# softmax(q) of batches 2 to 7: block transposes on VectorE with exchanged half rows, in place of TensorE transposes

## The chip, the cores and the metric

One NeuronCore of a Trainium2 chip. The metric is the device time of one execution in microseconds; the kernel before has a median of 920.75 us over three runs (920.45 to 921.54). The profiled execution is another run of the same kernel.

## What is computed

Eight batches (B = 8) of eight heads (H = 8), 576 tokens (S) and 64 channels per head (D), followed by a feed-forward layer with squared relu. All inputs are drawn in float32, the two weights come as float64 words. Cut to what matters:

```python
q_s = softmax of q over the 64 channels of a head (max, exp, sum + 1e-9, divide)
k_s = softmax of k over the 576 tokens (max, exp, sum + 1e-9, divide)
kv  = einsum('bhsd,bhse->bhde', k_s, v)
att = einsum('bhsd,bhde->bhse', q_s, kv)
x   = att.transpose(0, 2, 1, 3).reshape(B * S, H * D)      # 4608 x 512
h   = maximum(x @ w_in, 0)                                  # w_in 512 x 2048
out = h * h @ w_out                                         # w_out 2048 x 512
```

## The kernel before

Every large product is done three times in 32-bit pieces: an operand is cut into a rounded high part (a ScalarE copy) and a low part (a subtraction on VectorE or GpSimd), and high x high, high x low and low x high are added in PSUM.

The outer loop (line 634) runs over t = 0 to 8. In round t the feed-forward layer works on 512 tokens of batch t (round 8 takes the last 64 tokens of all eight batches, kept in DRAM as x_tail), and the attention of batch b = t + 1 is done beside it. The feed-forward layer has NF = 16 steps f. A step issues `first(t, f)` (12 matmuls of 512 columns into a PSUM tile h, of which there are two), then ScalarE's relu r and VectorE's square in place (L478, L479), and later `second(f - 2)` (12 matmuls into the accumulators acc). `split_g(f)` makes the two parts gh (ScalarE, L487) and gl (VectorE, L488) that `second(f)` reads; it is issued in step f after `second(f - 2)` in the program, from step 2 on. The h tile of step f is free for `first(f + 2)` once gl of step f is done.

The heads are taken in four pairs p = 0 to 3. Pair p has the four steps f = 4p to 4p + 3, called quarters i = 0 to 3 here. `step` (line 590) is issued between first and second, `step_after` (line 601) after split_g:

- quarter 0: exp of q (ScalarE), then row sums, 1e-9, reciprocal and the scaling into qn (VectorE, `q_exp`, `q_norm`); for p = 0 the same for the 64 tail rows of all heads (`tail_norm`).
- quarter 1: exp of k; the loads of k and q of the next pair are issued on SP's queue.
- quarter 2: `tail_turn` (p = 0 only, two TensorE transposes of the tail), `kv_product` (10 matmul instructions, then VectorE and ScalarE make kv, kvh, kvl), and `q_turn` (four TensorE transposes of qn into PSUM, qh by ScalarE, ql by VectorE); then the loads of v.
- quarter 3: `x_product` (6 matmuls of 288 columns, copied to x), and `prepare(b, p + 1)`: the maxima of k over a partition's rows (VectorE), the maximum across partitions and the subtraction (GpSimd), the row maxima of q and their subtraction (VectorE, `q_max`). For the next batch's pair 0, `prepare` is issued after the 16 steps.

q is loaded with four consecutive tokens on each partition, both heads of the pair side by side (256 KB in pieces of 1 KB); the 64 tail tokens of all heads come in a load of their own. Token order in x is therefore (partition, c), and `store` writes the rows of out by "(p c) e -> p c e".

Round 0 and the start before it are ordered by a planner (a cost model of the engines decides the order of each engine's instructions). From round 1 on the order is that of the program text (`manual_schedule`, line 636), and every engine and SP's DMA queue run their instructions in that order: an instruction that waits holds up all behind it. In the start (lines 520 to 572), batch 0 is done pair by pair in stages; `k_max` writes the tile km, of which there are two, and a TensorE transpose (`k_turn_max`, L320) reads it.

Of the kernel before, what the change touches and what calls it, by code (L numbers as in the profile page):

```python
# [9 lines left out]
F32 = mybir.dt.float32  # L10
F32R = mybir.dt.float32r
# [3 lines left out]
AF = mybir.ActivationFunctionType  # L15
ALU = mybir.AluOpType
AX = mybir.AxisListType
# [5 lines left out]
def attention_ffn(  # L23
# [19 lines left out]

    nc = tc.nc
    B, H, S, D = q.shape
    DM = H * D
    DF = w_in.shape[1]
    P = 128  # L50
    C = 4
    M = C * P
# [6 lines left out]
    EPS = 1e-9  # L59
# [2 lines left out]
    LW = 2  # L62
    LD = 6
    SH = S // 2
    assert B * TL == M and DM == NP * P and C * P == M

    const = ctx.enter_context(tc.tile_pool(name="const", bufs=1))
# [105 lines left out]
    made = {}  # L173
# [15 lines left out]
    def load_kq(b, p, which, queue=nc.sync):  # L189
# [4 lines left out]
        )  # L194
        made[which, b, p] = t

    def load_v(b, p):
        t = pair_tile(b, p, [P, VW], "v")[:, 0:C * W].rearrange("p (c w) -> p c w", c=C)
        nc.gpsimd.memset(t[:, :, D:D + 1], 1.0)
        for j in range(2):  # L200
            nc.sync.dma_start(
                out=t[:, :, j * (D + 1):j * (D + 1) + D],
                in_=v[b, 2 * p + j, 0:M, :].rearrange("(p c) d -> p c d", c=C),
            )
        made["v", b, p] = t

    def load_tail_kq(b, which, queue=nc.sync):

        src = k if which == "k" else q
        t = (att if b else boot).tile(  # L210
            [P, G, D], F32, tag=f"{which}t", name=f"{which}t_{b}", bufs=1
        )
        for g in range(2):
            queue.dma_start(
                out=t[g * TL:(g + 1) * TL],
                in_=src[b, g * G:(g + 1) * G, M:S, :].rearrange("h p d -> p h d"),
            )
        made[f"{which}t", b] = t
# [10 lines left out]

    def load_tail(b):  # L230
        load_tail_kq(b, "k")
        load_tail_kq(b, "q")

    def small(shape, tag, name, bufs=2):
        pool = att if shape[-1] % 64 == 0 else tiny
        return pool.tile(shape, F32, tag=tag, name=name, bufs=bufs)
# [8 lines left out]
    def rows_norm(t, g, name, eng, out=None):  # L245
        sm = small([P, g], f"sm_{g}", f"sm_{name}")
        nc.vector.tensor_reduce(out=sm, in_=t, op=ALU.add, axis=AX.X)
        nc.vector.tensor_scalar_add(sm, sm, EPS)
        nc.vector.reciprocal(out=sm, in_=sm)
        by = sm.unsqueeze(2).broadcast_to([P, g, D])  # L250
        if out is not None:
            t, by = (a.rearrange("p (h c) d -> p h c d", h=2) for a in (t, by))
        eng.tensor_tensor(out=t if out is None else out, in0=t, in1=by, op=ALU.mult)

    def tail_exp(b):
        qt = made["qt", b]
# [26 lines left out]
    def k_max(b, p):  # L283
        kr = made["k", b, p]
        tl, th = tail_of(b, p)
        km = small([P, P], "km", f"km_{b}_{p}")
        nc.vector.tensor_reduce(  # L287
            out=km.rearrange("p (h d) -> p h d", h=2), in_=kr.rearrange("p h c d -> p h d c"),
            op=ALU.max, axis=AX.X,
        )  # L290
        nc.vector.tensor_tensor(  # L291
            out=km[tl], in0=km[tl], in1=made["kt", b][tl, th, :].rearrange("p h d -> p (h d)"),
            op=ALU.max,
        )
        made["km", b, p] = km
# [20 lines left out]
    def k_turn_max(b, p):  # L316

        km = made.pop(("km", b, p))
        ps = bank(f"kmT_{b}_{p}")
        nc.tensor.transpose(out=ps[:, 0:P], in_=km, identity=ident)  # L320
        kc = small([P, 1], "kc", f"kc_{b}_{p}")
        nc.vector.tensor_reduce(out=kc, in_=ps[:, 0:P], op=ALU.max, axis=AX.X)
        dg = small([P, P], "dg", f"dg_{b}_{p}")
        nc.vector.tensor_scalar(
            out=dg, in0=ident, scalar1=kc, scalar2=None, op0=ALU.mult
        )
        made["dg", b, p] = dg
# [20 lines left out]
    def q_max(b, p, eng):  # L348
        rows_max(made["q", b, p].rearrange("p h c d -> p (h c) d"), 2 * C, f"{b}_{p}", eng)
# [5 lines left out]
    def q_norm(b, p, eng):  # L355
        qr = made.pop(("q", b, p)).rearrange("p h c d -> p (h c) d")
        qn = pair_tile(b, p, [P, C, P], "qn")
        rows_norm(
            qr, 2 * C, f"{b}_{p}", eng, qn.rearrange("p c (h d) -> p h c d", h=2)
        )  # L360
        made["qn", b, p] = qn
# [138 lines left out]
    def store(t, acc, c):  # L500
        o = cvt.tile([P, DM], F32, tag="w", name=f"o_{t}_{c}")
        if t == B and c == C - 1:
            nc.vector.tensor_copy(out=o[:, 0:DM // 2], in_=acc[c][:, 0:DM // 2])
            nc.scalar.copy(out=o[:, DM // 2:DM], in_=acc[c][:, DM // 2:DM])
        elif c % 2:
            nc.scalar.copy(out=o, in_=acc[c])
        else:
            nc.vector.tensor_copy(out=o, in_=acc[c])
        if t < B:
            rows = out[t * S:t * S + M, :].rearrange("(p c) e -> p c e", c=C)  # L510
            nc.sync.dma_start(out=rows[:, c, :], in_=o)
        else:
            per = P // TL
            for j in range(per):
                r0 = (c * per + j) * S + M
                queue = nc.scalar if c == C - 1 and j % 2 else nc.sync
                queue.dma_start(out=out[r0:r0 + TL, :], in_=o[j * TL:(j + 1) * TL, :])
# [63 lines left out]
    def prepare(b, p):  # L581

        k_max(b, p)
        if b > 1:
            k_shift_pool(b, p)
        q_max(b, p, nc.vector if b > 1 else nc.gpsimd)
        if p == 0:
            tail_exp(b)

    def step(b, s):  # L590

        p, i = divmod(s, NP)
        if i == 0:
            if b == 1:
                k_turn_max(b, p)
            q_exp(b, p)
            q_norm(b, p, nc.vector if b > 1 else nc.gpsimd)
            if p == 0:
                tail_norm(b)

    def step_after(b, s, x):

        p, i = divmod(s, NP)
        if b == 1 and s in (1, 4, 8, 12):
            k_shift_pe(b, p)
            k_exp(b, p)
        elif b > 1 and i == 1:
            k_exp(b, p)
        if i == 1:
            if p + 1 < NP:  # L610
                load_kq(b, p + 1, "k")
                load_kq(b, p + 1, "q")
            elif b + 1 < B:
                load_kq(b + 1, 0, "k")
                load_kq(b + 1, 0, "q")
        elif i == 2:
            if p == 0:
                tail_turn(b)
            kv_product(b, p)
            q_turn(b, p)  # L620
            if p + 1 < NP:
                load_v(b, p + 1)
            elif b + 1 < B:
                load_v(b + 1, 0)
                load_tail(b + 1)
                load_tail_v(b + 1)
        elif i == 3:
            x_product(b, p, x)
            if p + 1 < NP:
                prepare(b, p + 1)  # L630
# [77 lines left out]
```

## Time and profile before

| | before |
|---|---|
| median of 3 runs | 920.75 us |
| profiled execution, its own time | 920.5 us |
| span from first to last instruction | 918.7 us |
| granted TensorE clock, mean | 0.992 of 2.4 GHz |
| TensorE (PE) busy | 880.0 us, 96% |
| weight loads (PEld) busy | 731.2 us, 80% |
| VectorE (DVE) busy | 502.4 us, 55% |
| ScalarE (ACT) busy | 348.9 us, 38% |
| GpSimd (POOL) busy | 154.7 us, 17% |
| time outside the span | 1.8 us |

Busy shares are means over the whole span. Matmuls are pipelined, so the duration of one matmul in a row (0.39 us for 512 columns) is longer than the distance from one start to the next (0.227 us); what a matmul costs is read from the distances. Rounds 1 to 6, in which the changed code runs, lie between about 156 and 742 us. In rows of the timeline, x2 or x8 counts merged instructions, and what stands in brackets is idle time of that engine just before and what ended it.

### The profile page before, as it was taken

What the parts mean: (1) busy time and instruction counts of PE and PEld (TensorE: products, weight loads), DVE (VectorE), ACT (ScalarE), POOL (GpSimd) and SP (SyncE); (2) the same over time, 40 slices, a digit from 0 to 9 for tenths busy, and PEclk for the clock granted to TensorE, in tenths of its full rate; (3) what the DMA queues carried; (4) which work ended last, traced back from release to release, by engine and by line L of the source; (5) the groups of instructions that cost most, each with busy time, mean ns of one, the idle gap of its engine ahead of it and who ended that gap; (6) DMA issues with size and microseconds to landing.
All of it is one profiled execution on the core that took longest, in us unless ns stands there. A gap on an engine that the chain in (4) does not pass through costs nothing.

```text
span 918.7 us, 11463 instructions
## 1 busy us (share of the span) xinstructions
PE 880.0 (96%) x4136; PEld 731.2 (80%) x4136; DVE 502.4 (55%) x982; ACT 348.9 (38%) x679; POOL 154.7 (17%) x238
## 2 busy tenths in 40 slices
PE   3598999999999999999999999999999999999997
PEld 2486778888888888888888888888888888888886
DVE  8978888654564447545745466454744442233222
ACT  3997445333343234333433343333423332232221
POOL 3366663101111111111111101111110100000000
PEclk9799999999999999999999999999999999999999
DMA  8990102111221122111311031112211020001001
GB/s 247 355 381 25 38 24 84 35 35 34 59 81 35 35 53 86 35 34 32 95 36 35 15 101 35 35 35 58 81 35 35 1 97 1 1 8 39 0 1 47
DMA packets 84937, 57.38 MB, mean 62 GB/s; under 512 B 53520, under 2 KB 78096, under 8 KB 84752
## 3 DMA queue, kind: packets, MB, share of 16 engines
q1 hardware_dynamic: 83168, 55.33, 19.6%
q10 hardware_dynamic: 1712, 1.31, 0.5%
q8 instruction: 33, 0.54, 0.2%
q14 instruction: 24, 0.20, 0.1%
HBM read 46.14 MB, written 10.49 MB: 62 GB/s over the span
## 4 chain that ended last, share of the span: by engine, by line
PE 81%; DVE 8%; ACT 7%; issue 2%; DMA 1%; POOL 1%; SPq 0%; DVEq 0%; ACTq 0%
PE h L473 38%; PE acc L495 37%; PE kv L391 2%; PE x L428 2%; PE qT L368 1%; DVE xl L464 1%; DVE gl L488 1%; ACT r L478 1%; DVE h L479 1%; ACT gh L487 1%; ACT raw_i L125 1%; ACT raw_i L126 1%; ACT raw_o L125 1%; DVE km L287 1%; ACT raw_o L126 1%
## 5 line engine op out<-in xcount | busy, mean ns | idle before, releaser
L473 PE MATMUL h<-xh,wi 128*128 128x512 f32 x1152 | 382.8, 395 | 5.3 <-ACT wi L152 5.0
L495 PE MATMUL acc<-wo,gh 128*128 128x512 f32 x1152 | 349.6, 390 | 3.5 <-ACT gh L487 3.4
L473 PEld LDWEIGHTS h<-xh,wi 128*128 128x128 f32 x1152 | 217.1, 189 | 53.1 <-ACT wi L152 5.9
L495 PEld LDWEIGHTS acc<-wo,gh 128*128 128x128 f32 x1152 | 215.1, 188 | 49.7 <-ACT gh L487 5.7
L473 PE MATMUL h<-xl,wi 128*128 128x512 f32 x576 | 225.7, 392 | 0.0
L495 PE MATMUL acc<-wo,gl 128*128 128x512 f32 x576 | 217.4, 389 | 0.0
L479 DVE SCALAR_TENSOR_TENSOR h<-h,r 128x512 f32<-128x512 f32 x144 | 100.6, 698 | 193.4 <-ACT r L478 192.7
L488 DVE TENSOR_TENSOR gl<-h,gh 128x512 fp32r<-128x512 f32 x144 | 99.5, 691 | 171.5 <-ACT gh L487 168.1
L478 ACT ACTIVATE r<-h 128x512 f32<-128x512 f32 x144 | 86.0, 597 | 219.2 <-PE h L473 219.1
L487 ACT ACTIVATE gh<-r 128x512 fp32r<-128x512 f32 x144 | 91.0, 632 | 196.8 <-PE acc L495 194.1
L495 PEld LDWEIGHTS acc<-wo,gl 128*128 128x128 f32 x576 | 108.0, 188 | 22.6
L473 PEld LDWEIGHTS h<-xl,wi 128*128 128x128 f32 x576 | 108.9, 189 | 20.8
L301 POOL TENSOR_TENSOR k<-k,kmx 128x512 f32<-128x512 f32 x24 | 31.0, 1291 | 172.6 <-issue 172.6
L313 POOL PARTITION_ALL_REDUCE kmx<-km x24 | 17.6, 734 | 226.8 <-DVE km L291 221.1
L391 PEld LDWEIGHTS kv<-v,ek 128*128 128x128 f32 x256 | 33.4, 195 | 4.5 <-ACT wi L152 2.4
L391 PE MATMUL kv<-v,ek 128*128 128x129 f32 x256 | 34.8, 279 | 2.2 <-ACT wi L152 2.0
L287 DVE TENSOR_REDUCE km<-k 128x128 f32<-128x512 f32 x32 | 33.9, 1059 | 2.7 <-DMA k<-in_k_dram 2.7
L342 ACT ACTIVATE ek<-k 128x512 f32<-128x512 f32 x32 | 20.1, 627 | 23.6 <-POOL k L301 16.7
L382 DVE TENSOR_TENSOR ql<-qT,qh 128x512 fp32r<-128x512 f32 x32 | 22.0, 688 | 6.8 <-ACT qh L381 6.8
L416 ACT CAST kvh<-kv 128x128 fp32r<-128x128 f32 x32 | 9.5, 298 | 39.3 <-DVE kv L406 39.1
L240 DVE TENSOR_REDUCE mx<-q 128x8 f32<-128x512 f32 x32 | 21.7, 679 | 2.7 <-DMA q<-in_q_dram 2.3
L464 DVE TENSOR_TENSOR xl<-x,xh 128x512 fp32r<-128x512 f32 x32 | 20.2, 687 | 5.4 <-ACT xh L463 5.3
(84 smaller groups left out, 675.2 us busy)
## 6 DMA issues: line engine op xcount, KB each, us to landing
k<-in_k_dram SPq DMA_DIRECT2D x32, 256.0 KB, 2.8
v<-in_v_dram SPq DMA_DIRECT2D x64, 128.0 KB, 3.1
raw_i<-in_moe_w_in_dram SPq DMA_DIRECT2D x16, 512.0 KB, 8.1
raw_o<-in_moe_w_out_dram SPq DMA_DIRECT2D x16, 512.0 KB, 7.9
out_dram<-o SPq DMA_DIRECT2D x32, 256.0 KB, 2.6
q<-in_q_dram SPq DMA_DIRECT2D x28, 256.0 KB, 2.9
q<-in_q_dram ACTq DMA_DIRECT2D x4, 256.0 KB, 4.7
kt<-in_k_dram SPq DMA_DIRECT2D x16, 64.0 KB, 2.7
```

The costliest lines, as they stand in the source:

```text
L240: nc.vector.tensor_reduce(out=mx, in_=t, op=ALU.max, axis=AX.X)
L287: nc.vector.tensor_reduce(out=km.rearrange("p (h d) -> p h d", h=2), in_=kr.rearrange("p h c d -> p h d c"), op=ALU.max, axis=AX.X,)
L301: eng.tensor_tensor(out=kr, in0=kr, in1=kmx.rearrange("p (h d) -> p h d", h=2).unsqueeze(2).broadcast_to([P, 2, C, D]), op=ALU.subtract,)
L382: nc.vector.tensor_tensor(out=ql[:, 0:M], in0=ps, in1=qh[:, 0:M], op=ALU.subtract)
L391: nc.tensor.matmul(out=ps[:, 0:W], lhsT=kr[:, c, :], rhs=vr[:, c, :], start=(c == 0), stop=False)
L464: nc.vector.tensor_tensor(out=lo, in0=src[:, p, :], in1=hi, op=ALU.subtract)
L473: nc.tensor.matmul(out=ps, lhsT=w[f][:, p * P:(p + 1) * P], rhs=m, start=(n == 0), stop=(n == 3 * NP - 1))
L478: nc.scalar.activation(out=r, in_=ps, func=AF.Relu)
L479: nc.vector.scalar_tensor_tensor(out=ps, in0=ps, scalar=0.0, in1=r, op0=ALU.max, op1=ALU.mult)
L487: nc.scalar.activation(out=gh, in_=r, func=AF.Square)
L488: nc.vector.tensor_tensor(out=gl, in0=ps, in1=gh, op=ALU.subtract)
L495: nc.tensor.matmul(out=acc[c], lhsT=a[:, cs], rhs=w[f], start=(f == 0 and n == 0), stop=(f == NF - 1 and n == 2),)
```

## The change

For batches b >= TB = 2 only. q of a pair is loaded by four DMAs into a tile of 128 partitions x 18 x 32: partition j*64 + a*32 + r holds, for head j and channel half a, the 32 channels of token 32 g + r, for g = 0 to 17, so that all 576 tokens are in it and the separate tail load of q is left out. A row of a head lies on two partitions, so row maxima and row sums of the halves are exchanged with four small SBUF-to-SBUF DMAs (`swap_halves`, 32 partitions x 72 bytes each) and joined. VectorE then transposes the tile in 32 x 32 blocks into 128 partitions (channels) x 576 tokens; ScalarE makes the high part, GpSimd the low part. Tail transposes, the copies of the tail and the TensorE transposes of q are not issued for these batches. Tokens of x are now in their natural order, so `store` writes "(c p) e -> p c e" for t >= 2. For all batches the tile km of `k_max` has one buffer in place of two.

By place: `blocks_max` stands in `prepare` (quarter 3 of the pair before), `blocks_exp` in quarter 0, `blocks_norm` in quarter 1 (both in `step`), `blocks_turn` in quarter 1 (in `step_after`, ahead of the loads of the next pair), `blocks_split` in quarter 2 (in `step`).

```diff
@@ -62,6 +64,9 @@
     LW = 2
     LD = 6
     SH = S // 2
+    TB = 2
+    Q = 32
+    NG = S // Q
     assert B * TL == M and DM == NP * P and C * P == M
 
     const = ctx.enter_context(tc.tile_pool(name="const", bufs=1))
@@ -194,6 +199,24 @@
         )
         made[which, b, p] = t
 
+    def load_q_blocks(b, p):
+
+        t = att.tile([P, NG, Q], F32, tag="q", name=f"q_{b}_{p}")
+        for j in range(2):
+            for a in range(2):
+                at = j * D + a * Q
+                nc.sync.dma_start(
+                    out=t[at:at + Q],
+                    in_=q[b, 2 * p + j, :, a * Q:(a + 1) * Q].rearrange("(g t) d -> t g d", t=Q),
+                )
+        made["q", b, p] = t
+
+    def load_q(b, p):
+        if b < TB:
+            load_kq(b, p, "q")
+        else:
+            load_q_blocks(b, p)
+
     def load_v(b, p):
         t = pair_tile(b, p, [P, VW], "v")[:, 0:C * W].rearrange("p (c w) -> p c w", c=C)
         nc.gpsimd.memset(t[:, :, D:D + 1], 1.0)
@@ -229,7 +252,8 @@
 
     def load_tail(b):
         load_tail_kq(b, "k")
-        load_tail_kq(b, "q")
+        if b < TB:
+            load_tail_kq(b, "q")
 
     def small(shape, tag, name, bufs=2):
         pool = att if shape[-1] % 64 == 0 else tiny
@@ -252,6 +276,58 @@
             t, by = (a.rearrange("p (h c) d -> p h c d", h=2) for a in (t, by))
         eng.tensor_tensor(out=t if out is None else out, in0=t, in1=by, op=ALU.mult)
 
+    def swap_halves(t, name):
+
+        o = small([P, NG], "sw", f"sw_{name}", 1)
+        for j in range(2):
+            for a in range(2):
+                at, of = j * D + a * Q, j * D + (1 - a) * Q
+                nc.sync.dma_start(out=o[at:at + Q], in_=t[of:of + Q])
+        return o
+
+    def blocks_max(b, p):
+        mx = small([P, NG], "bmx", f"bmx_{b}_{p}", 1)
+        nc.vector.tensor_reduce(out=mx, in_=made["q", b, p], op=ALU.max, axis=AX.X)
+        made["bmx", b, p] = mx, swap_halves(mx, f"m_{b}_{p}")
+
+    def blocks_exp(b, p):
+        t = made["q", b, p]
+        mx, sw = made.pop(("bmx", b, p))
+        nc.vector.tensor_tensor(out=mx, in0=mx, in1=sw, op=ALU.max)
+        nc.vector.tensor_tensor(
+            out=t, in0=t, in1=mx.unsqueeze(2).broadcast_to([P, NG, Q]), op=ALU.subtract
+        )
+        nc.scalar.activation(out=t, in_=t, func=AF.Exp)
+        sm = small([P, NG], "bsm", f"bsm_{b}_{p}", 1)
+        nc.vector.tensor_reduce(out=sm, in_=t, op=ALU.add, axis=AX.X)
+        made["bsm", b, p] = sm, swap_halves(sm, f"s_{b}_{p}")
+
+    def blocks_norm(b, p):
+        t = made["q", b, p]
+        sm, sw = made.pop(("bsm", b, p))
+        nc.vector.scalar_tensor_tensor(
+            out=sm, in0=sm, scalar=EPS, in1=sw, op0=ALU.add, op1=ALU.add
+        )
+        nc.vector.reciprocal(out=sm, in_=sm)
+        nc.vector.tensor_tensor(
+            out=t, in0=t, in1=sm.unsqueeze(2).broadcast_to([P, NG, Q]), op=ALU.mult
+        )
+
+    def blocks_turn(b, p):
+
+        t = made.pop(("q", b, p)).rearrange("p g d -> p (g d)")
+        qt = att.tile([P, S], F32, tag="qn", name=f"qT_{b}_{p}")
+        nc.vector.transpose(out=qt, in_=t)
+        made["qf", b, p] = qt
+
+    def blocks_split(b, p):
+        qt = made.pop(("qf", b, p))
+        qh = att.tile([P, S], F32R, tag="qh", name=f"qh_{b}_{p}", bufs=1)
+        ql = att.tile([P, S], F32R, tag="ql", name=f"ql_{b}_{p}", bufs=1)
+        nc.scalar.copy(out=qh, in_=qt)
+        nc.gpsimd.tensor_tensor(out=ql, in0=qt, in1=qh, op=ALU.subtract)
+        made["qT", b, p] = (qh, ql)
+
     def tail_exp(b):
         qt = made["qt", b]
         rows_max(qt, G, f"t{b}", nc.vector)
@@ -283,7 +359,7 @@
     def k_max(b, p):
         kr = made["k", b, p]
         tl, th = tail_of(b, p)
-        km = small([P, P], "km", f"km_{b}_{p}")
+        km = small([P, P], "km", f"km_{b}_{p}", 1)
         nc.vector.tensor_reduce(
             out=km.rearrange("p (h d) -> p h d", h=2), in_=kr.rearrange("p h c d -> p h d c"),
             op=ALU.max, axis=AX.X,
@@ -507,7 +583,9 @@
         else:
             nc.vector.tensor_copy(out=o, in_=acc[c])
         if t < B:
-            rows = out[t * S:t * S + M, :].rearrange("(p c) e -> p c e", c=C)
+            rows = out[t * S:t * S + M, :].rearrange(
+                "(p c) e -> p c e" if t < TB else "(c p) e -> p c e", c=C
+            )
             nc.sync.dma_start(out=rows[:, c, :], in_=o)
         else:
             per = P // TL
@@ -583,18 +661,27 @@
         k_max(b, p)
         if b > 1:
             k_shift_pool(b, p)
-        q_max(b, p, nc.vector if b > 1 else nc.gpsimd)
+        if b >= TB:
+            blocks_max(b, p)
+            return
+        q_max(b, p, nc.gpsimd)
         if p == 0:
             tail_exp(b)
 
     def step(b, s):
 
         p, i = divmod(s, NP)
-        if i == 0:
-            if b == 1:
-                k_turn_max(b, p)
+        if b >= TB:
+            if i == 0:
+                blocks_exp(b, p)
+            elif i == 1:
+                blocks_norm(b, p)
+            elif i == 2:
+                blocks_split(b, p)
+        elif i == 0:
+            k_turn_max(b, p)
             q_exp(b, p)
-            q_norm(b, p, nc.vector if b > 1 else nc.gpsimd)
+            q_norm(b, p, nc.gpsimd)
             if p == 0:
                 tail_norm(b)
 
@@ -607,17 +694,22 @@
         elif b > 1 and i == 1:
             k_exp(b, p)
         if i == 1:
+            if b >= TB:
+                blocks_turn(b, p)
             if p + 1 < NP:
                 load_kq(b, p + 1, "k")
-                load_kq(b, p + 1, "q")
+                load_q(b, p + 1)
             elif b + 1 < B:
                 load_kq(b + 1, 0, "k")
-                load_kq(b + 1, 0, "q")
+                load_q(b + 1, 0)
         elif i == 2:
-            if p == 0:
-                tail_turn(b)
-            kv_product(b, p)
-            q_turn(b, p)
+            if b >= TB:
+                kv_product(b, p)
+            else:
+                if p == 0:
+                    tail_turn(b)
+                kv_product(b, p)
+                q_turn(b, p)
             if p + 1 < NP:
                 load_v(b, p + 1)
             elif b + 1 < B:
```

## Rows read from the trace of the kernel before

**Rows 1.** The page: busy time of each engine, share of the span, instructions.
```profile
PE 880.0 (96%) x4136; PEld 731.2 (80%) x4136; DVE 502.4 (55%) x982; ACT 348.9 (38%) x679; POOL 154.7 (17%) x238
```
**Rows 2.** The page: chain that ended last, shares of the span by engine.
```profile
PE 81%; DVE 8%; ACT 7%; issue 2%; DMA 1%; POOL 1%; SPq 0%; DVEq 0%; ACTq 0%
```
**Rows 3.** Timeline of PE, quarter 2 of an ordinary pair: start, duration, instruction.
```profile
286.55 1.05 PE L391 MATMUL kv<-v,ek 128*128 128x129 f32 x8
287.44 0.39 PE L394 MATMUL kv<-v_tail,kt 128*128 128x129 f32 x2
287.66 0.60 PE L368 MATMUL qT<-ident,qn 128*128 128x128 f32 x4
288.02 0.48 PE L473 MATMUL h<-xh,wi 128*128 128x512 f32 x1
288.34 0.39 PE L473 MATMUL h<-xl,wi 128*128 128x512 f32 x1
288.57 0.62 PE L473 MATMUL h<-xh,wi 128*128 128x512 f32 x2
```
**Rows 4.** Timeline of PE, first pair of a batch, quarters 2 and 3.
```profile
261.64 0.38 PE L268 MATMUL qTt<-ident,qt 128*128 128x128 f32 x2
261.85 1.06 PE L391 MATMUL kv<-v,ek 128*128 128x129 f32 x8
262.75 0.39 PE L394 MATMUL kv<-v_tail,kt 128*128 128x129 f32 x2
263.42 0.66 PE L368 MATMUL qT<-ident,qn 128*128 128x128 f32 x4 [0.29 <-DVE qtl L276]
...
269.40 0.29 PE L428 MATMUL x<-qh,kvh 128*128 128x288 f32 x1
```
**Rows 5.** Timeline of PE, third step of a round.
```profile
255.62 0.94 PE L473 MATMUL h<-xh,wi 128*128 128x512 f32 x2
```
**Rows 6.** Waits of weight loads, 150 to 900 us: in total, times, longest.
```profile
PEld qT L368 <- DVE qtl L276: 3.0, 6, 0.6
PEld h L473 <- DVE gl L488: 2.4, 5, 0.5
```
**Rows 7.** Groups by line and form: count, busy us, mean ns.
```profile
L301 POOL TENSOR_TENSOR k<-k,kmx 128x512 f32<-128x512 f32 x24 | 31.0, 1291 | 172.6 <-issue 172.6
...
L247 DVE TENSOR_REDUCE sm<-q 128x8 f32<-128x512 f32 x32 | 21.8, 681 | 0.6
...
L353 ACT ACTIVATE q<-q 128x512 f32<-128x512 f32 x32 | 20.1, 629 | 6.4 <-POOL q L241 5.1
...
L249 DVE RECIPROCAL sm<-sm 128x8 f32<-128x8 f32 x32 | 6.4, 201 | 0.9
```
**Rows 8.** Timeline of DVE, first pair's quarter 2, then quarters 3 and 0.
```profile
264.50 0.29 DVE L417 TENSOR_TENSOR kvl<-kv,kvh 128x128 fp32r<-128x128 f32 x1 [0.36 <-ACT kvh L416]
...
272.30 0.67 DVE L240 TENSOR_REDUCE mx<-q 128x8 f32<-128x512 f32 x1
...
276.37 0.69 DVE L488 TENSOR_TENSOR gl<-h,gh 128x512 fp32r<-128x512 f32 x1
```
**Rows 9.** Timeline of PEld, the weight load that opens the step two later.
```profile
280.89 0.19 PEld L473 LDWEIGHTS h<-xh,wi 128*128 128x128 f32 x1
```
**Rows 10.** Timeline of SP's queue: DMA issues.
```profile
242.23 2.56 SPq L223 DMA_DIRECT2D v_tail<-in_v_dram  x4
...
282.32 0.37 SPq L192 DMA_DIRECT2D k<-in_k_dram  x1
```
**Rows 11.** DMA issues by line: count, KB each, median us to landing.
```profile
v<-in_v_dram SPq DMA_DIRECT2D x64, 128.0 KB, 3.1
...
v_tail<-in_v_dram SPq DMA_DIRECT2D x32, 32.0 KB, 2.3
```
**Rows 12.** Timeline of DVE in the start, a pair's maxima of k.
```profile
13.21 1.02 DVE L287 TENSOR_REDUCE km<-k 128x128 f32<-128x512 f32 x1
```
**Rows 13.** Timeline of PE in the start, the transpose that reads km.
```profile
14.61 0.47 PE L320 MATMUL kmT<-ident,km 128*128 128x128 f32 x1 [3.50 <-DVE km L291]
```

## The prediction

> **What bounds the kernel now.** I read the page's busy times first: TensorE is busy 96% of the span, no other engine over 55% [rows 1]. The chain of waits agrees, with 81% of the span on TensorE [rows 2]. Then I read the timeline of TensorE in rounds 1 to 6, where the changed code runs. There a matmul of 512 columns starts 0.23 us after the one before it, and the attention's products stand between them without a gap [rows 3]. In that stretch TensorE idles in two places only. In the first pair of a batch the transposes of q wait for VectorE's qtl, and in the third step of a round the weight load of h waits for gl of the first step [rows 6]. So time is won there by taking instructions or these waits from TensorE, and lost where another engine makes TensorE wait. Last I read VectorE, ScalarE and SP's queue around quarters 3, 0 and 1, to see how much room the new chain has.
>
> **What leaves TensorE.** (a) The four transposes qT: the first starts at 287.66, the first matmul of h behind them at 288.02 [rows 3], so 0.36 us a pair; 6 batches of 4 pairs make 24, so 8.6 us. (b) Behind them the second h matmul starts 0.32 us after the first (288.34 - 288.02), where the next distance is 0.23 (288.57 - 288.34) [rows 3]. These 0.09 us may go or come again behind the kv matmuls, which are short too: 0 to 2.2 us over 24 pairs; no row nearer, I take half, 1.1. (c) In the first pair the two tail transposes go, 261.85 - 261.64 = 0.21 us, and the wait behind kv: kv's last two start at 262.75 and take 0.22 together (287.44 to 287.66 [rows 3]), so the transposes could start at 262.97 and start at 263.42 [rows 4], 0.45 us. Six batches: 4.0 us. (d) In the third step of a round two h matmuls take 0.94 us [rows 5] where two take 0.62 [rows 3], 0.32 us, for gl of the first step is late, five times [rows 6]. Before that, VectorE does the subtraction of q and two instructions of the tail in `prepare`, ahead of the copies of acc and of that step's square; all three move or go, some 1.5 us of VectorE work (0.69 for a pass of 512, as gl [rows 8], and two of half the width). So I let the stall go: 0 to 1.6 us, taken as 1.5. Sum: 8.6 + 1.1 + 4.0 + 1.5 = 15.2 us; 12.6 at least if nothing gets in the way, 16.4 at most.
>
> **What the change adds, and what hides it.** VectorE loses ql (0.69) and the tail passes and gains one block transpose; its passes grow from 512 to 576 columns. As a sum that is nothing at 55% busy. What counts is that it waits in order, first for a swap of maxima (`blocks_exp`), then for a swap of sums (`blocks_norm`); behind it stand gl, the transpose and the next step's square.
>
> *Length of a swap.* No row shows a DMA from SBUF to SBUF. Four tail loads of v, the smallest transfers of the trace, are issued in 2.56 us, 0.64 each, and one load of k takes 0.37 [rows 10]; the tail loads land after 2.3 us [rows 11]. Four small issues, the last landing 2.3 us after its start: 3 x 0.64 + 2.3 = 4.2 us, or 3 x 0.37 + 2.3 = 3.4. I take 4.2, as the transfers nearest in size. That the landing of the four overlaps is shown by the same tail loads.
>
> *Quarter 0 of an ordinary pair* (18 in all; times of this trace). The maximum over 576 columns starts at 272.30 and takes 0.67 x 576/512 = 0.76, to 273.1. The swap ends at 277.3. Then the joined maximum 0.2 (a small instruction is 0.20 [rows 7]), the subtraction 0.78 (0.69 x 576/512), exp 0.71 (from 0.629), the sum 0.77 (from 0.681) [rows 7], gl 0.69: 280.45, where gl ended at 277.06 before [rows 8]. The first to need it is the weight load of h two steps on, at 280.89 [rows 9]. So 0.4 us of room, 1.2 with the shorter swap: no stall, but this is the tight place of the change.
>
> *Quarter 1.* The sums end at 279.8, their swap at 284.0; joining, reciprocal and scaling take 0.2 + 0.2 + 0.78, gl 0.69: 285.9. It is needed when the h matmuls behind kv begin, at 288.02 less the transposes, about 287.5 after the change; 1.5 us of room. Then the block transpose, which has no row: between a pass of 512 scaled up, 0.77, and a reduce that reads across its tile, 1.02 [rows 12] x 576/512 = 1.15; I take 0.77, as it reads a row in order. It ends at 286.6, ScalarE's qh at 287.3, GpSimd's ql, 1.29 x 576/512 = 1.45 [rows 7], at 288.8; the x product that reads them comes at about 293.
>
> *First pair of a batch.* The first two steps of a round have no second matmuls between, so this is tighter. By the same steps the swap of sums ends at about 262.1, the transpose at 264.1, and kvl, queued behind it, comes at 267.5, where it came at 264.8 [rows 8]. The x product stood at 269.40 [rows 4] and comes 1.4 us earlier by (a), (c) and (d): 268.0. Room 0.5 us. The Trainium skill (VectorE: DVE Perf Modes, "The three transpose paths") has 311 ns for a 128x128 block transpose of 16-bit elements; 4.5 of them are an estimate of 1.40 us, by which the first pairs would lose 0.13 us each and the sum 0.8 us. No row here shows it.
>
> *Loads of q.* They wait for the block transpose, three to four microseconds later than before, and move 2304 pieces of 128 bytes. A load of v has 512 pieces (128 partitions x 4) and lands after 3.1 us, a tail load has 128 and lands after 2.3 [rows 11]: 2.1 ns a piece. Four issues of 0.64 from 286.6, the last landing after 2.3 + 448 x 0.0021 = 3.2: 291.7. The next maximum over q is due 24 us after 272.30, at 296: hidden with 4 us to spare, 1.5 us in the first pair. The loads of v, queued behind them on SP, are needed a whole pair later; the stores of a round come behind the swap of maxima and read accumulators that are not wanted before step 2.
>
> *One buffer for km.* In steady rounds 24 us lie between two uses: nothing. In the start the maximum of the last pair begins at 13.21 [rows 12], but the transpose that reads the pair before runs at 14.61 for 0.47 [rows 13]: 1.9 us late at most; VectorE has other pairs' work there, and the planner will order round 0 anew, with a gain as likely as a loss of that size. Cost -1.9 to 1.9; I take 0.9 lost, half of the shown delay.
>
> Sum: 15.2 - 0.9 = 14.3 us gained. The profiled execution took 920.5 (span 918.7 and 1.8 around it), 0.25 below the median of the runs shown; 920.5 - 14.3 = 906.2 is what I predict. Its own range: 920.5 - 16.4 - 1.9 = 902.2 to 920.5 - 12.6 + 1.9 = 909.8, say 902 to 910.
>
> **The rivals.**
>
> *The swap is the new bound, and the kernel slower.* Each us by which a swap exceeds 4.2 + 0.4 = 4.6 us makes the h weight load wait in 18 pairs. From 15.2/18 = 0.85 us more, 5.4 us, all is lost. With 6.0 us (0.9 for an issue, 3.3 for a landing) the stall is 1.4 x 18 = 25 us: 920.5 - 14.3 + 25 = 931. For it: no row of such a transfer, four in a row on one queue, twice a pair. Against: the tail loads, four in a row too, land after 2.3 us. Chance 0.15.
>
> *The same, in part.* A swap of about 5 us: 0.4 x 18 = 7 us lost, 913 to 914. Every term of quarter 0 that I scaled from 512 columns adds to it. Chance 0.17, for 910 to 920.
>
> *The 128-byte pieces of q come late.* If the four loads followed one another and a piece cost double, 2304 x 4.2 ns + 2 us = 11.7 us from 286.6: 298.3, 2.3 us after the maximum is due; the swap behind it starts that much later, quarter 0 stalls 1.9 us x 18 = 34 us: 940. For it: the trace has no piece under 256 bytes. Against: pieces of 256 bytes (v) land 0.8 us after loads with a quarter of the pieces. Chance 0.07. The Trainium skill (DMA: Bandwidth & Descriptors, "Specifications") asks for 512 bytes or more for full rate, with a read-modify-write below; by it the load is slow, and whether that shows hangs on the 4 us of room.
>
> *The planner makes round 0 worse* by 4 to 8 us, on top of the gain: 912. For it: round 0 has its own waits, and one buffer goes. Against: nothing else in its work changes but the last loads and maxima. Chance 0.06.
>
> **Numbers.** The forecast has 0.55. The range of 8 in 10 takes in the partial stall and the planner: 901 to 921; outside lie the two slow rivals, 0.22 less what they hold below 921. About 0.2%, 1.8 us, is what a measurement can tell from no change. Faster: 0.55 + 0.06 + most of the partial stall = 0.76; same 0.05; slower 0.19.
>
> **What would show it.** In an ordinary pair the h matmuls stand right behind kv, and the period of a pair is 0.36 to 0.45 us shorter; in the first pair kv is preceded by no transposes and followed by no wait. VectorE idles before the joined maximum and before the joined sums, waiting for DMA, some 2.5 to 3 us each, without a wait of weight loads for gl. If these weight loads wait in quarter 2, the swap was too long; if VectorE idles before the maximum over q, the loads were. A round 0 that ends later or earlier would be the planner's.

## The result, and the profile after

| | before | after |
|---|---|---|
| median, runs side by side | 921.14 us (920.45 to 924.20, 4 runs) | 911.52 us (910.61 to 912.09, 4 runs) |
| profiled execution, its own time | 920.5 us | 910.61 us |
| span | 918.7 us | 908.7 us |
| granted TensorE clock, mean | 0.992 | 0.992 |
| ratio of after to before | | 0.9887, 95% 0.9867 to 0.9908 |

The change makes the kernel 1.1% faster. The prediction was 906.2 us, with a range of 901 to 921: the time is in the range, but 1.5 us beyond the forecast's own 902 to 910. The spans of the two profiled executions differ by 10.0 us, where 14.3 were forecast, and the question is where 4 us went.

First the page of after: the busy times, then the chain's shares by engine ([rows 1, 2] are their like).

```profile
PE 873.0 (96%) x4028; PEld 720.8 (79%) x4028; DVE 493.2 (54%) x964; ACT 347.6 (38%) x667; POOL 176.7 (19%) x214
...
PE 88%; ACT 3%; DMA 3%; DVE 2%; SPq 2%; issue 1%; POOL 1%; DVEq 0%
```

TensorE lost 108 records, the transposes, and is still what bounds the kernel. The waits of weight loads from 150 to 900 us, in the columns of [rows 6], have neither of the two waits that stood there; the two that are left are new and belong to one place, the first step of round 1.

```profile
PEld h L549 <- ACT xh L539: 1.5, 1, 1.5
PEld h L549 <- DVE xl L540: 0.5, 1, 0.5
```

The timeline of TensorE in quarter 2 of an ordinary pair answers [rows 3] (columns: start, duration, engine, line, operation, count):

```profile
285.07 1.05 PE L467 MATMUL kv<-v,ek 128*128 128x129 f32 x8
285.96 0.39 PE L470 MATMUL kv<-v_tail,kt 128*128 128x129 f32 x2
286.10 0.48 PE L549 MATMUL h<-xh,wi 128*128 128x512 f32 x1
286.42 0.40 PE L549 MATMUL h<-xl,wi 128*128 128x512 f32 x1
286.65 0.63 PE L549 MATMUL h<-xh,wi 128*128 128x512 f32 x2
```

The first h stands 0.14 us behind the start of kv's last two; before it stood 0.58 behind it (287.44 to 288.02 [rows 3]). That is 0.44 a pair. In the first pair of a batch, the like of [rows 4], h follows as closely, with no transposes ahead and no wait:

```profile
261.31 1.05 PE L467 MATMUL kv<-v,ek 128*128 128x129 f32 x8
262.20 0.39 PE L470 MATMUL kv<-v_tail,kt 128*128 128x129 f32 x2
262.34 0.48 PE L549 MATMUL h<-xh,wi 128*128 128x512 f32 x1
```

The third step of a round shows no late gl: two h matmuls take 0.62 us where they took 0.94 [rows 5].

```profile
255.64 0.62 PE L549 MATMUL h<-xh,wi 128*128 128x512 f32 x2
```

VectorE in quarters 0 and 1 of an ordinary pair (the brackets hold its idle time just before, and what ended it; sw_m and sw_s are the tiles that the swaps write; beside [rows 8]):

```profile
294.69 0.75 DVE L290 TENSOR_REDUCE bmx<-q 128x18 f32<-128x576 f32 x1
...
299.27 0.18 DVE L296 TENSOR_TENSOR bmx<-bmx,sw_m 128x18 f32<-128x18 f32 x1 [2.51 <-DMA sw_m<-bmx]
299.48 0.76 DVE L297 TENSOR_TENSOR q<-q,bmx 128x576 f32<-128x576 f32 x1
...
301.67 0.68 DVE L564 TENSOR_TENSOR gl<-h,gh 128x512 fp32r<-128x512 f32 x1
...
305.44 0.18 DVE L308 SCALAR_TENSOR_TENSOR bsm<-bsm,sw_s 128x18 f32<-128x18 f32 x1 [2.48 <-DMA sw_s<-bsm]
...
307.22 0.77 DVE L320 STREAM_TRANSPOSE qT<-q 128x576 f32<-128x576 f32 x1
```

From the end of the maximum (294.69 + 0.75 = 295.44) to the joined maximum a swap takes 3.8 us, 2.5 of them idle. gl ends at 302.35. The weight load that needs it, the like of [rows 9], starts at 303.17: 0.8 us of room.

```profile
303.17 0.19 PEld L549 LDWEIGHTS h<-xh,wi 128*128 128x128 f32 x1
```

Last the transfers (count, KB each, median us to landing, as in [rows 11]):

```profile
q<-in_q_dram SPq DMA_DIRECT2D x96, 72.0 KB, 2.4
...
sw_m<-bmx SPq DMA_DIRECT2D x96, 2.2 KB, 1.7
```

**Where the 10.0 us are.** From the times at which the first matmul of h of each round starts, in TensorE's timeline:

| round | before, length | after, length | difference |
|---|---|---|---|
| 2 starts at | 250.41 | 250.39 | 0.0 |
| 2 to 6, each | 97.83 | 95.58 | -2.25 |
| 7 | 87.04 | 87.73 | +0.69 |
| 8 | 92.1 | 92.7 | +0.6 |

Round 7 has no attention beside it, and of the change only the new order of the stored rows runs in it; yet it is 0.69 us longer. That is the first thing to explain. The second is that round 1, which has the change, brought nothing by the start of round 2. The first matmul of acc in round 1 already stands 1.9 us later; the second line is of the kernel before:

```profile
163.01 0.62 PE L571 MATMUL acc<-wo,gh 128*128 128x512 f32 x2
...
161.14 0.62 PE L495 MATMUL acc<-wo,gh 128*128 128x512 f32 x2
```

### The profile page after: what moved, and what is told of

Same layout as the page of the kernel before. It is cut to its first block, busy times and chain, and to the rows that moved or that the text cites. A ratio compares the mean times of both kernels' runs of the same rounds, so it can differ in the third digit from the quotient of the medians.

```text
span 908.7 us, 11603 instructions
## 1 busy us (share of the span) xinstructions
PE 873.0 (96%) x4028; PEld 720.8 (79%) x4028; DVE 493.2 (54%) x964; ACT 347.6 (38%) x667; POOL 176.7 (19%) x214
## 4 chain that ended last, share of the span: by engine, by line
PE 88%; ACT 3%; DMA 3%; DVE 2%; SPq 2%; issue 1%; POOL 1%; DVEq 0%
PE acc L571 41%; PE h L549 41%; PE kv L467 3%; PE x L504 2%; DMA raw_o<-in_moe_w_out_dram 1%; DMA v_tail<-in_v_dram 1%; DMA q<-in_q_dram 1%; SPq L117 1%; PE kv L470 1%; DMA k<-in_k_dram 1%; ACT raw_i L130 1%; SPq L224 0%; ACT raw_o L130 0%; POOL w_o L148 0%; DVE w_o L141 0%
## 5 line engine op out<-in xcount | busy, mean ns | idle before, releaser
L328 POOL TENSOR_TENSOR ql<-qT,qh 128x576 fp32r<-128x576 f32 x24 | 34.1, 1420 | 102.1 <-issue 53.8
L300 ACT ACTIVATE q<-q 128x576 f32<-128x576 f32 x24 | 16.5, 686 | 86.6 <-DVE q L297 84.8
L308 DVE SCALAR_TENSOR_TENSOR bsm<-bsm,sw_s 128x18 f32<-128x18 f32 x24 | 4.3, 178 | 62.1 <-DMA sw_s<-bsm 62.1
L327 ACT CAST qh<-qT 128x576 fp32r<-128x576 f32 x24 | 16.2, 674 | 39.7 <-DVE qT L320 39.7
L296 DVE TENSOR_TENSOR bmx<-bmx,sw_m 128x18 f32<-128x18 f32 x24 | 4.2, 176 | 44.5 <-DMA sw_m<-bmx 44.5
```

The lines of the kernel that those rows point to most:

```text
L328: nc.gpsimd.tensor_tensor(out=ql, in0=qt, in1=qh, op=ALU.subtract)
```

## The experiments

**What makes round 7 longer?** In after's round 7, a step of 12 h matmuls takes 2.72 us (782.73 to 785.45) when it is step 11, and 2.79 when it is step 12 (788.18 to 790.97): 0.227 us a matmul, then 0.233.

```profile
782.73 0.39 PE L549 MATMUL h<-xh,wi 128*128 128x512 f32 x1
...
785.45 0.62 PE L571 MATMUL acc<-wo,gh 128*128 128x512 f32 x2
...
788.18 0.39 PE L549 MATMUL h<-xh,wi 128*128 128x512 f32 x1
...
790.97 0.62 PE L571 MATMUL acc<-wo,gh 128*128 128x512 f32 x2
```

Weights of steps 12 to 15 (LATE = 12) lie in a pool of their own, `late`, which comes behind the small tiles in SBUF. The change adds three tiles of 72 bytes a partition, each in a slot of 96: in the built programs `late` starts at byte 190720 of a partition before, a multiple of 256, and at 191008 after, 32 bytes past a multiple of 64 and of 256. Theory A: it is this place. The rival: something of the change that still runs, such as queues, transfers or the order of the stored rows. The first kernel widens one small tile and so moves `late` on by 32 bytes:

```diff
-        sm = small([P, NG], "bsm", f"bsm_{b}_{p}", 1)
+        sm = small([P, Q], "bsm", f"bsm_{b}_{p}", 1)[:, 0:NG]
```

> The changed kernel with one small tile widened by 56 bytes of row (bsm from 18 to 32 columns), so that the tiles placed behind it, among them the weights of steps 12 to 15, start on a multiple of 64 bytes again (they stand 32 bytes off in the changed kernel). Theory A, the place of these weights makes their matmuls slower (0.233 us for 0.227): pace 0.227 in all steps, every round about 0.6 us shorter, 9 rounds, so 911.5 - 5.5 = 906 us. Rival B, contention with the small DMAs or with VectorE: pace and time stay, 911.5 us.

Measured: 910.54 us (910.20 to 912.84), ratio to before 0.9896 (0.9879 to 0.9914). A miss: round 7 stayed at 87.70, and step 12 still takes 2.80 us.

```profile
787.74 0.40 PE L549 MATMUL h<-xh,wi 128*128 128x512 f32 x1
...
790.54 0.62 PE L571 MATMUL acc<-wo,gh 128*128 128x512 f32 x2
```

Its `late` starts at 191040, 64 bytes past a multiple of 256. Either theory A is wrong or 64 is not enough. The opposite test moves `late` of the kernel before by 32 bytes and changes nothing else:

```diff
     tiny.tile([P, 32], F32, tag="pad2", name="pad2")
+    tiny.tile([P, 8], F32, tag="pad3", name="pad3")
```

> The kernel before with a 32-byte tile added ahead of the same tiles, so that they stand 32 bytes off there too; nothing else changes and no small DMA is added. Theory A: the matmuls of steps 12 to 15 take 0.233 us in every round, 920.8 + 5.5 = 926 us. Rival B: 920.8 us.

Measured: 925.19 us (924.14 to 925.59), ratio 1.0048 (1.0033 to 1.0063); round 7 takes 87.71 and the attention rounds 98.16 to 98.21. This shows theory A without any other part of the change: the place of tiles alone costs 4.9 us. The pad moves the tiles of the start too, which use the same bytes before `late` does: of the 5.1 us between the two traces, 3.6 lie in rounds 1 to 8 and 1.5 ahead of them. Then the same on the kernel after, with a smaller pad, so that `late` starts at 190976, a multiple of 256:

```diff
-    tiny.tile([P, 32], F32, tag="pad2", name="pad2")
+    tiny.tile([P, 24], F32, tag="pad2", name="pad2")
```

> The changed kernel with an unused tile 32 bytes smaller, so that the weights of steps 12 to 15 start on a multiple of 256 bytes as in the kernel before (in e1_aligned they start 64 bytes beyond one, and their matmuls stayed at 0.233 us). Theory A, sharpened: the place within 256 bytes decides; pace 0.227 in all steps, round 7 87.0 us long for 87.7, and 5 us less than e1_aligned, 905 to 906 us. Rival B, the slower pace has another cause in the change: round 7 stays at 87.7 and the time at 910.5.

Measured: 907.43 us (906.77 to 907.85), ratio 0.9843 (0.9830 to 0.9856). Round 7 takes 87.04 again, attention rounds 95.04 (one 95.81, one 95.1), and step 12 takes 2.72:

```profile
786.40 0.39 PE L549 MATMUL h<-xh,wi 128*128 128x512 f32 x1
...
789.12 0.62 PE L571 MATMUL acc<-wo,gh 128*128 128x512 f32 x2
```

So the place cost the change 0.54 us in each attention round, and 4 to 4.5 us in all. Round 7 of all thirteen traces says the same: matmuls of steps 12 to 15 start 0.227 us apart in the seven kernels whose `late` starts at a multiple of 256, and about 0.233 apart in the six where it starts 32, 64 or 128 bytes past one. This holds for h, where the tile in `late` is loaded as weights, and for acc, where it is the operand that streams past them.

**One buffer for km, and round 0.** The kernel before with that edit alone:

```diff
-        km = small([P, P], "km", f"km_{b}_{p}")
+        km = small([P, P], "km", f"km_{b}_{p}", 1)
```

> The kernel before with one buffer for km, the part of the change that touches the start. Theory C, the single buffer lengthens the start and round 0: round 1 or 2 begins 1.5 to 2.2 us later and the time is 922 to 923 us. Rival D, the loss in round 0 comes from the new loads and maxima at its end, or from the order that the planner finds: 920.8 us, within 0.5.

Measured: 924.63 us (921.77 to 926.55), ratio 1.0051 (1.0032 to 1.0070), more than either theory had. Its profiled execution took 921.77, the least of its four, and starts round 2 at 251.88, 1.5 us later than before. So the edit costs something here; the runs spread too much to say how much. The first kernel with two buffers for km again, and one for kmx in their place so that all tiles fit:

```diff
-        km = small([P, P], "km", f"km_{b}_{p}", 1)
+        km = small([P, P], "km", f"km_{b}_{p}")
...
-        kmx = small([P, P], "kmx", f"kmx_{b}_{p}")
+        kmx = small([P, P], "kmx", f"kmx_{b}_{p}", 1)
```

> As e1_aligned, with two buffers for km again and one for kmx (which is used from batch 2 on only, with 24 us between uses) so that it fits. Theory C: about 1.5 to 2 us less than e1_aligned, 904 to 904.5 us. Rival D: as e1_aligned, 906 us.

Measured: 910.19 us (909.38 to 911.32), ratio 0.9888 (0.9873 to 0.9903), which can't be told from 910.54 with one buffer. Its four executions differ in the mean granted clock: two at 0.992 took 909.4 and 909.7 us, two at 0.989 took 910.7 and 911.3; all four with one buffer had 0.992. The same two edits on the kernel with `late` at a multiple of 256:

> As e7_aligned256, with two buffers for km and one for kmx: the order of the start is then that of the kernel before. If the single buffer costs the start what is missing there (about 2 us), 903.5 us; if not (as e4_aligned_km2 beside e1_aligned), as e7_aligned256.

Measured: 905.84 us (905.33 to 906.54), ratio 0.9827 (0.9814 to 0.9841): the fastest of all, 1.6 us under the one with one buffer (whose runs took 906.77 to 907.85). The traces agree on what the buffer changes. In after, and in the kernels of the change with one buffer, the planner puts the last x product of round 0 at its very end (154.01 in after, 149.48 before), so that the first step of round 1 waits for its copy:

```profile
156.22 0.50 PE L549 MATMUL h<-xh,wi 128*128 128x512 f32 x1 [1.25 <-ACT xh L539]
156.94 0.50 PE L549 MATMUL h<-xl,wi 128*128 128x512 f32 x1 [0.22 <-DVE xl L540]
```

With two buffers the product stands at 150.87 and these waits are gone. (In the kernel before with one buffer it stands at 150.46, so that kernel's 1.5 us are something else.) In the traces of the two aligned kernels round 2 starts 1.1 us earlier (250.50 with one buffer, 249.41 with two; this row is of two):

```profile
249.41 0.39 PE L549 MATMUL h<-xh,wi 128*128 128x512 f32 x1
```

By its own gain in round 1 (0.42 x 3 + 1.15 = 2.4, below) this kernel should be there at 250.41 - 2.4 = 248.0; 1.4 us are still missing. To see whether these are round 0's, the last kernel of this row keeps batch 2 as before and changes batches 3 to 7 alone, so that the program is the old one up to the end of round 1:

```diff
-    TB = 2
+    TB = 3
...
-        q_max(b, p, nc.gpsimd)
+        q_max(b, p, nc.vector if b > 1 else nc.gpsimd)
...
```

> As e8_aligned256_km2, but the change applies from batch 3 on (TB = 3): start and round 0 then run instruction by instruction in the order of the kernel before, and round 1 works as before. Theory H, what the change loses before round 2 (about 2.2 us: it ought to gain that much in round 1, and round 2 begins at the same time) comes from another order of round 0: round 2 begins at 250.4, the gain is that of five rounds, 920.5 - 5 x 2.9 = 906 us, within 1 us of e7_aligned256. Rival: the start and round 0 are not the cause, and e9_from_batch3 is 2.9 us slower than e8_aligned256_km2.

Measured: 906.99 us (905.80 to 908.67), ratio 0.9840 (0.9825 to 0.9856); round 2 starts at 250.58, within 0.2 of before, and the rounds behind it take 95.04. With round 0's work unchanged nothing is lost ahead of round 2. So the loss comes with what the change makes of round 0.

The 1.4 us that two buffers leave are not in the order of its instructions. The kernel with two further DMAs a swap (below) runs the same instructions as the fastest one, in the same order on TensorE, VectorE, ScalarE and GpSimd, up to the first matmul of acc in round 1. It has that matmul at 161.35 us, 0.2 behind the kernel before; the fastest has it at 162.53. In round 0 both wait some 1.9 us ahead of a kv. In the fastest kernel's trace the next matmuls are slow; these are its lines, then those of the other:

```profile
116.84 1.18 PE L467 MATMUL kv<-v,ek 128*128 128x129 f32 x8 [1.97 <-ACT wi L157]
...
119.10 2.97 PE L571 MATMUL acc<-wo,gh 128*128 128x512 f32 x8
...
117.40 1.13 PE L469 MATMUL kv<-v,ek 128*128 128x129 f32 x8 [1.92 <-ACT wi L156]
...
119.06 2.00 PE L573 MATMUL acc<-wo,gh 128*128 128x512 f32 x8
```

From 118 to 123 us the granted clock (last but two) is 0.68 of 2.4 GHz in the first, that is in part at the lower level of 1.2, and 1.00 in the second:

```profile
118.00:123.00 5.00, 5.00 (x18) 0.68 0.23 52
...
118.00:123.00 5.00, 5.00 (x27) 1.00 0.23 52
```

0.32 of 5 us is an estimate of 1.6 us lost, enough for the 1.4. Three of the four traces with two buffers and the change from batch 2 on have this stretch at 0.66 to 0.68; all others have 1.00 there. Why it falls in some and not in others is open.

**How much room has the swap?** The next kernel takes away the exchange of halves and is otherwise the first kernel (a pad of 96 bytes in place of the swaps' tile keeps `late` where it was):

```diff
-        made["bmx", b, p] = mx, swap_halves(mx, f"m_{b}_{p}")
+        made["bmx", b, p] = mx, mx
...
-        made["bsm", b, p] = sm, swap_halves(sm, f"s_{b}_{p}")
+        made["bsm", b, p] = sm, sm
```

> As e1_aligned, without any swap: each half row is normalised by its own maximum and sum, so the exchange of the halves is left out of the computation (the two VectorE instructions that join them still run, on the own half twice). Theory E: the swaps cost nothing as they stand, so the same time as e1_aligned, 906 us, within 0.5. Rival G, the waits for the swaps cost part of the missing gain: 2 us or more less than e1_aligned.

Measured: 910.66 us (909.83 to 910.89), ratio 0.9893 (0.9876 to 0.9909), against 910.54 with the swaps. 48 swaps with 192 DMAs and some 2.5 us of idle VectorE each cost nothing that can be measured. The other direction puts further small DMAs ahead of each swap on the queue, three at first, on the kernel after:

```diff
         o = small([P, NG], "sw", f"sw_{name}", 1)
+        w = small([P, 24], "junk", f"junk_{name}", 1)
+        for i in range(3):
+            nc.sync.dma_start(out=w[i * Q:(i + 1) * Q, 0:NG], in_=t[i * Q:(i + 1) * Q])
```

> As e1_aligned (weights on a multiple of 64 bytes), with three more small DMAs of 32 partitions x 72 bytes issued ahead of the four of every swap into a tile that nobody reads, so that every swap ends about 1.9 us later (0.62 us an issue in the trace of the changed kernel). Theory E, the swap has about 1 us of room in quarter 0 and about 1 us in the first pair, and beyond it TensorE waits: 0.9 us in 18 pairs and 1 to 2 us in 6 first pairs, 906 + 16 + 6 to 12 = 928 to 934 us, with weight loads of h waiting for gl. Rival F, the swap is hidden anyway: 906 to 908 us.

Measured: 965.81 us (964.32 to 969.58), ratio 1.0497 (1.0471 to 1.0523). The sign is right, the size a miss: 54 us more than after, where the expectation had 22 to 28 us of waits. Most swaps take 5.6 to 6.0 us, 13 of 47 longer, up to 7.5. The waits of weight loads from 260 to 780 us:

```profile
PEld h L552 <- DVE gl L567: 25.0, 26, 2.3
...
PEld x L507 <- ACT kvh L495: 14.3, 5, 3.2
```

The expectation had the first of these in quarter 0 alone; half of them (13 of 26, 6.2 us) come behind the second swap, in quarter 1. The second is the first pair of a batch, where both swaps lie within one pair's chain: the x product waits up to 3.2 us for kvh, which VectorE's kv makes behind the second swap. And a wait can cost more than its length. The next line and three windows hold the first wait for kvh of that stretch (columns of the windows: stretch, us; busy us and instructions of TensorE, weight loads, VectorE, ScalarE, GpSimd; granted clock; DMA share; GB/s). After 1.83 busy us in four, TensorE runs the next 10 us at a mean granted clock of 0.83 of 2.4 GHz, that is in part at the lower level of 1.2; an estimate from 0.17 of 10 us is 1.7 us lost on top of the wait of 2.81. The two waits above are 39.3 of the 54 us, the clock some 7 (mean 0.988 from 250 to 800 us); the rest is not taken apart.

```profile
280.63 0.40 PE L507 MATMUL x<-qh,kvh 128*128 128x288 f32 x1 [2.81 <-ACT kvh L495]
...
276.00:280.00 4.00, 1.83 (x9) 1.17 (x7) 3.15 (x8) 1.20 (x2) 1.45 (x2) 1.00 0.40 87
280.00:290.00 10.00, 9.37 (x36) 7.74 (x37) 4.83 (x10) 2.53 (x6) 0.72 (x1) 0.83 0.20 38
290.00:300.00 10.00, 10.00 (x48) 8.34 (x47) 3.86 (x8) 3.69 (x7) 1.72 (x2) 1.00 0.10 28
```

Two kernels then look for the break-even on the fastest kernel, with one and with two such DMAs (`range(1)` and `range(2)` in the same edit; the new tile of 96 bytes takes the place of the pad):

```diff
-    tiny.tile([P, 24], F32, tag="pad2", name="pad2")
...
+        for i in range(1):
```

> As e8_aligned256_km2 with one more small DMA (read by nobody) ahead of the four of each swap, 0.62 us more a swap. Theory E with the rooms of the trace of e8_aligned256_km2 (quarter 0: gl ends 1.0 us before the weight load of h behind it; first pair: kvh ends 1.0 us before the x product's weight load, and both swaps add up there): no wait in the 18 ordinary pairs except behind a swap that is late anyway (one in six takes 4.2 to 5.5 us for 3.8), 0.2 to 0.5 us in the first pairs: 905.8 + 2 to 4 = 908 to 910 us. Rival: what made e5_long_swap so slow (965.8 us) is there from the first added DMA on: 920 us or more.

Measured: 910.47 us (908.97 to 911.77), ratio 0.9878 (0.9854 to 0.9902), 0.5 us over the expected 908 to 910, with swaps of 4.4 us (five of the 24 of sums take 5.8 to 6.3). Waits from 250 to 790 us:

```profile
PEld x L506 <- ACT kvh L494: 3.0, 3, 1.6
PEld h L551 <- DVE gl L566: 2.5, 7, 0.7
```

> As e10_swap_plus1 with two more small DMAs a swap, 1.24 us. Theory E: 0.25 us in 18 ordinary pairs, 1.5 us in 6 first pairs, and in the first pairs a lower granted clock behind the wait as in e5_long_swap (0.83 over 10 us behind a wait of 2.8 us): 905.8 + 4.5 + 9 = 919 us, up to 928 us with the clock. Rival, a straight line from no delay to e5_long_swap: 905.8 + 2/3 x 55 = 942 us.

Measured: 932.84 us (929.86 to 933.25), ratio 1.0112 (1.0080 to 1.0144), with swaps of 5.0 us (one in three 5.3 to 6.8); more than was expected. The same waits:

```profile
PEld h L551 <- DVE gl L566: 12.5, 16, 1.3
PEld x L506 <- ACT kvh L494: 9.7, 5, 2.7
```

0.6 us more a swap cost 4.6 us, the next 0.6 cost 22. The two waits add up to 22.2 us, of the 27.0 by which this kernel is slower than the one without further DMAs. Between the two, on a straight line, the kernel is as slow as before at 4.4 + 0.6 x (921.2 - 910.5) / (932.8 - 910.5) = 4.7 us.

## Why the prediction was right, and by how much

**The instructions taken from TensorE, (a) to (c).** Right, to a tenth. (a) and (b) were 0.36 + 0.045 a pair, and 0.42 to 0.44 is measured (pair period 24.18 before, 23.76 after). The second part is right for another reason: the stumble of 0.32 us from the first to the second h, which (b) hoped to halve, is still there (286.10 to 286.42). What went is 0.08 of kv's last two, which the transposes had stretched to 0.22 and which now take 0.14. (c) was 0.66 a batch; in the first pair the distance from kv's last two to h fell from 1.08 (262.75 [rows 4] to 263.83) to 0.14, and the tail transposes' 0.21 went too, together 1.15, so 0.73 beyond the ordinary pair's 0.42. The line of the kernel before that ends the 1.08:

```profile
263.83 0.47 PE L473 MATMUL h<-xh,wi 128*128 128x512 f32 x1
```

**(d) The third step's stall.** Gone, as predicted: 0.32 us, in five rounds.

With `late` on a multiple of 256 an attention round takes 95.04 us for 97.83: 2.8 us, times five, and 2.4 in round 1, which has no (d): 16.4, where the sum had 15.2 and 16.4 at most.

**The swap.** Its length was predicted as 4.2 us, with 3.4 as the other end, and is 3.6 to 3.9 in most places; of the 42 that VectorE waits for in after, five take 4.4 to 4.8 (up to 5.5 in the aligned kernels). Issues stand 0.63 us apart, as taken, but land after 1.7 us, not 2.3. The room in quarter 0 was predicted as 0.4 beyond the swap of 4.2, and is 0.8 beyond one of 3.8: the same point, 4.6. The steps behind it were right to hundredths: subtraction 0.76 (0.78), sum 0.75 (0.77), gl 0.68 (0.69). In the first pair kvl was predicted to end at 267.5 and the x product to come at 268.0; they stand at 267.1 and 267.9. So the rival of a swap that bounds the kernel failed on its condition alone; its mechanism exists and the last three kernels show it. Its price was too low. The prediction counted only quarter 0 of 18 ordinary pairs and had the break-even at 5.4 us; it is about 4.7, as the first pairs pay for both swaps, with 9.7 of the 22.2 us of waits; with still longer swaps the clock adds to it. The partial rival (910 to 920) covers the measured time, but not by its mechanism: no weight load waits for gl in rounds 2 to 6 of after, and taking the swaps out gains nothing. So it is luck in part that the time lies in the stated range of 901 to 921: the range was that wide for other causes than the one that cost most.

**Block transpose.** Taken as 0.77 us; it is 0.771, mean of 24. The Trainium skill's figure for 16-bit elements (VectorE: DVE Perf Modes, "The three transpose paths"), scaled to this tile, was an estimate of 1.40; the trace does not bear it out for 32-bit elements, which go as fast as a plain pass.

```profile
L320 DVE STREAM_TRANSPOSE qT<-q 128x576 f32<-128x576 f32 x24 | 18.5, 771 | 0.6
```

**Loads of q.** In time: they land after 2.4 us, where 3.2 were taken, and VectorE does not wait for them in rounds 1 to 6. Pieces of 128 bytes stand under the 512 bytes that the Trainium skill (DMA: Bandwidth & Descriptors, "Specifications") wants for full rate; no lateness shows at four loads of 72 KB a pair.

**What failed.** The sum had no term for where tiles lie in SBUF. Counted from the traces: 16.4 us won in rounds 1 to 6 (5 x 2.79 + 2.4), 4.5 lost by `late` (0.54 in each of six rounds, 0.69 and 0.6 in rounds 7 and 8), 1.9 lost ahead of round 1 (163.01 for 161.14, above): 10.0, as measured. The second failure is the size of one term: "I take 0.9 lost" for km and the planner's new order; it is 1.9 in after's trace, at the bound that the prediction gave, but not where it put it. No late kmT decides: the first matmul of acc in round 0 stands at 50.59, for 50.55 before. Most of it is the wait behind an x product that the planner moved to the end of round 0 (1.25 + 0.22 of idle TensorE).

**Open.** Why weights at 32, 64 or 128 bytes past a multiple of 256 make matmuls 2.8% slower (128 is from the kernel with three further DMAs, whose round 7 takes 87.76); why the first kernel's attention rounds are 0.16 us shorter than after's with both off it; why TensorE's clock falls in round 0 in three of four traces with two buffers, which blurs what the buffer is worth (1.6 us in one pair of kernels, nothing that can be told in the other); and why one buffer makes the kernel before slower.

## What to carry to other kernels

Any new tile moves all tiles behind it: when matmul operands lie behind a pool of small tiles, compare the pace of a stretch that the change does not touch, and pad until their base is at a multiple of 256 bytes again, as it was here. A small exchange by DMA can be free on an engine that waits in order, but count its room where two exchanges fall into one chain, not only in the ordinary step. What is left here is in the fastest kernel: the change, 32 bytes less pad and two buffers for km (one for kmx), 905.84 us. When two traces differ by 1 or 2 us, look at the granted clock stretch by stretch before the order of instructions is blamed.

## What was not expected of the hardware

- Matmuls of 512 columns on 32-bit pieces start 0.233 us apart instead of 0.227 when the tiles of the layer's weights start 32, 64 or 128 bytes past a multiple of 256 bytes of a partition. 32 bytes of padding cost 4.9 us of 920.
- Four SBUF-to-SBUF DMAs of 2.2 KB on one queue are usable some 3.8 us after the data (issues 0.63 apart, the last landing after 1.7); five or six of 42 such swaps took 4.2 to 5.5.
- After 2.81 us of waiting the granted clock of TensorE was 0.83 over the next 10 us, so that a wait cost more than it lasted. After waits of 1.97 and 1.92 us at the same place in two programs of the same order it was 0.68 and 1.00 over 5 us.
